# Retention followed by a snake feed-forward layer on one core: later tiles in the natural layout, 64x64 array tiles and a written-out plan

## The chip, the cores and the metric

The kernel runs on one core of one Trainium2 chip. The metric is the device time of one execution in microseconds (us). The changed kernel's time stands against that of the kernel before.

## The reference

Four batches (B), eight heads (H), 768 tokens (S), head size 64 (D). Per batch and head a state of 64x64 decays and takes in one outer product per token; the output is the query times the state. The outputs, heads side by side, are x with 3072 rows of 512, which goes through a feed-forward layer of width 2048.

```
gamma = 1.0 - 2.0 ** (-5.0 - np.arange(H))
for t in range(S):
    state = gamma * state + einsum('bhd,bhe->bhde', k[:, :, t], v[:, :, t])
    y[:, :, t] = 1/sqrt(D) * einsum('bhd,bhde->bhe', q[:, :, t], state)
x = y.transpose(0, 2, 1, 3).reshape(B * S, H * D)
h = x @ w_in
s = sin(alpha * h)
g = h + s * s / (alpha + 1e-09)
out = g @ w_out
```

Inputs and output are float32.

## The kernel before

The tokens are cut into 24 tiles of 128 (six chunks in each of four batches). The list `order` takes the four first chunks first, then the rest batch by batch; "tile n" below is entry n of it. Tiles 0 to 3 are first chunks, 4 to 8 chunks 1 to 5 of batch 0, 9 to 13 those of batch 1, and so on.

**Feed-forward.** Groups of tiles go through it: group 0 has tiles 0 to 3, groups 1 to 10 two tiles each. A `Slot` multiplies w_in's columns of one block f of 128 (two blocks at a time from group 1 on) with the group's x (line 567, `ph`; four matmuls per block), ACT takes the sine (570), ACT or DVE squares (575, 577), DVE adds (582) into `gT`. `ff_out` multiplies `gT` with w_out (592, `po`; 16 matmuls of 512 columns per tile). `ph` and `po` of later groups share four PSUM banks. `phase` runs group g's eight slots between the `po` matmuls of group g-1, and calls the attention of the tiles to come at fixed slots: `score` and `blend` say where, and each tile is spread over a few slots.

**Attention.** A tile needs q and k with the head size on partitions (`qkT`). Tiles 0 to 7 are transposed on PE (`turn_half`, 247 and 249; `half_T`, `stage_T`), tiles 8 and later by a DMA transpose that SyncE issues (`turn`, 284). A *narrow* tile (0 to 9) forms its scores in eight matmuls with 64 rows and 128 columns of the array (`stage_A`, 293); then `stage_M` adds the state's part (332, 128 rows with zeros in `s_bd`), the scores' part (336), and the new state (312). A *wide* tile (10 and later, except first chunks) is loaded with two token halves on one partition and half of the heads in each half of the partitions (`load_seq`); its matmuls use the array as four tiles of 64x64, and `burst` issues one tile's blending, the next one's scores and the state together: `inter` (397), `scores` (413), `part` (433), `mix` (510), 64 small matmuls. Tiles 10 and 14 are wide with whole chunks; the others go in halves of 64 tokens (`fine`). DVE masks the scores (421), adds the state (462, 470), and scales the result into x (`xT`, 528); ACT, for the last batch GpSimd, copies the state to bf16 (438).

**Loads.** GpSimd issues all loads that cast to bf16: `load_chunk` (91, 98: 128 partitions, 64-element pieces), `load_seq` (121: 64 partitions, one head each), `load_w_in` (131) and `load_w_out` (134), four of each over 128 partitions. Its queue also scales v (155) and some decay tables (223). DMAs of this queue go in turn over eight semaphores, so each waits for the landing of the one eight places before. SyncE issues the first q and k, the DMA transposes and the output stores (607), in the order in which they are written.

**Order.** `tc.manual_schedule()` keeps each engine's instructions in the order of the program text: the first part (tiles 0 to 2, with `idle_work` on PE in between), group 0 written out by hand (`w[..]`, `F(ts, lo, hi)`), then the phases.

Of the kernel before, what the change touches and what calls it, by code (L numbers as in the profile page):

```python
# [11 lines left out]
ALU = mybir.AluOpType  # L12


@with_exitstack
def kernel(
# [10 lines left out]

# [37 lines left out]
    w_in_v = moe_w_in.rearrange("(ko ki) f -> ki ko f", ki=128)  # L65
    w_out_v = moe_w_out.rearrange("(fo fi) n -> fi fo n", fi=128)
    raw = {}

# [12 lines left out]
    def load_chunk(j, names="qkv"):  # L81
        for name, src in (("q", q), ("k", k), ("v", v)):
            if name not in names:
                continue
            if name == "v":
                t = big.tile([128, H, D], BF16, name="vr", tag="vr", bufs=10)
            elif name == "q" and paired(j):
                if "pairs" not in raw:
                    raw["pairs"] = work.tile([64, B, H, 2, D], BF16, name="qp", tag="gT", bufs=2)
                t = raw["pairs"][:, order.index(j)]  # L90
                nc.gpsimd.dma_start(out=t.rearrange("i h f d -> i h (f d)"), in_=pairs_of(src, j))
                raw[name, j] = t
                continue
            else:
                if ("qk", j) not in raw:
                    raw["qk", j] = big.tile([128, 2, H, D], BF16, name="qkr", tag="qkr", bufs=9)
                t = raw["qk", j][:, "qk".index(name)]
# [3 lines left out]
    whole = NCH + 2, 2 * NCH + 1  # L101

    def wide(j):
        return j >= NCH + 2 and j % NCH > 0

    def load_seq(bt, names="qkv", hs=range(H)):

        cs = [c for c in range(NCH) if wide(bt * NCH + c)]
        nh = 2 * len(cs)
        if "q" in names and hs[0] == 0:  # L110
            raw["seq", bt] = (big.tile([128, nh, 2, NP, D], BF16, name=f"qk_seq{bt}"),
                              big.tile([128, nh, NP, D], BF16, name=f"v_seq{bt}"))
        tqk, tv = raw["seq", bt]
        for name, src in (("q", q), ("k", k), ("v", v)):
            if name not in names:
                continue
            for h in hs:
                r = slice(64 * (h // NP), 64 * (h // NP) + 64)
                x = h % NP ^ h // NP
                o = tv[r, :, h % NP, :] if name == "v" else tqk[r, :, "qk".index(name), x, :]  # L120
                nc.gpsimd.dma_start(out=o, in_=src[bt, h, cs[0] * C:, :].rearrange("(f i) d -> i f d", i=64))  # L121
        for i, c in enumerate(cs):
            j, f = bt * NCH + c, slice(2 * i, 2 * i + 2)
            raw["qk", j], raw["k", j], raw["v", j] = tqk[:, f], tqk[:, f, 1], tv[:, f]

    WP = 4
    fw = d_ff // WP
    fo = FF // WP

    def load_w_in(i):  # L130
        nc.gpsimd.dma_start(out=w_in[:, :, i * fw:(i + 1) * fw], in_=w_in_v[:, :, i * fw:(i + 1) * fw])

    def load_w_out(i):
        nc.gpsimd.dma_start(out=w_out[:, i * fo:(i + 1) * fo, :], in_=w_out_v[:, i * fo:(i + 1) * fo, :])
# [3 lines left out]
    for name, src in (("q", q), ("k", k)):  # L138
# [4 lines left out]
    nc.sync.dma_start(out=alpha_row, in_=moe_alpha.rearrange("(fo fi) -> fo fi", fi=128))  # L143

    tio = consts.tile([128, C], F32, name="tio")
    nc.gpsimd.iota(tio, pattern=[[1, C]], channel_multiplier=0, base=0, allow_small_or_imprecise_dtypes=True)
    pos = consts.tile([128, NCH], F32, name="pos")
    nc.gpsimd.iota(pos, pattern=[[C, NCH]], channel_multiplier=1, base=0, allow_small_or_imprecise_dtypes=True)


    def scale_v(j, eng):
        t, by = raw["v", j], kg
        if wide(j):
            t, by = t.rearrange("i f p d -> i (f p) d"), kgq
        eng.tensor_mul(t, t, by[:, j % NCH, :, None].to_broadcast([128, H, D]))  # L155

    load_chunk(0, "v")
    load_chunk(order[1])
    load_chunk(order[2])
    load_w_in(0)  # L160
    load_w_in(1)


    warm = consts.tile([128, 512], F32, name="warm")
    nc.vector.memset(warm, 0.0)  # L165
    tiny = consts.tile([128, 1], F32, name="tiny")
    nc.scalar.activation(out=tiny, in_=warm[:, 0:1], func=ACTF.Exp)
    lg = consts.tile([128, H], F32, name="lg")
    for h in range(H):
        nc.vector.memset(lg[:, h:h + 1], lng[h])  # L170
    back = consts.tile([128, H], F32, name="back")
    far = consts.tile([128, C], F32, name="far")
    nc.vector.tensor_scalar(back, lg, pos[:, 0:1], -1.0, op0=ALU.mult, op1=ALU.mult)
    nc.vector.tensor_scalar(far, tio, pos[:, 0:1], 1e6, op0=ALU.is_lt, op1=ALU.mult)
    nc.vector.tensor_scalar_add(back, back, lscale)
    nc.vector.tensor_add(far, far, tio)
    dec = consts.tile([128, 2, NP, C], F32, name="dec")
    for h in range(H):
        nc.scalar.activation(out=dec[:, h % 2, h // 2, :], in_=far, func=ACTF.Exp, scale=lng[h], bias=back[:, h:h + 1])
    ident = consts.tile([128, 128], BF16, name="ident")  # L180
    nc.vector.tensor_scalar(ident, tio, pos[:, 0:1], None, op0=ALU.is_equal)
    lgp = consts.tile([128, NP], F32, name="lgp")
    for p in range(NP):
        for e in range(2):
            nc.vector.memset(lgp[64 * e:64 * e + 64, p:p + 1], lng[2 * p + e])

    expo = consts.tile([128, NCH, H], F32, name="expo")
    nc.vector.tensor_mul(expo, pos[:, :, None].to_broadcast([128, NCH, H]),
                         lg[:, None, :].to_broadcast([128, NCH, H]))
    mask01 = consts.tile([128, 128], BF16, name="mask01")  # L190
    mask_bc = mask01[:, None, :].to_broadcast([128, H, 128])
    kgq = consts.tile([128, NCH, H], F32, name="kgq")
    expoq = consts.tile([128, NCH, H], F32, name="expoq")
    tok = consts.tile([128, NCH, 2], F32, name="tok")
    lgq = consts.tile([128, NP], F32, name="lgq")
    maskq = consts.tile([128, 192], BF16, name="maskq")

    def half_table(b):
        r = slice(64 * b, 64 * b + 64)
        for f in range(2):  # L200
            nc.vector.tensor_scalar_add(tok[r, :, f], pos[r, :], float(64 * (f - b)))
        nc.vector.tensor_copy(lgq[r], lg[r, NP * b:NP * b + NP])

    def later_tables():
        for f in range(2):
            nc.vector.tensor_mul(expoq[:, :, NP * f:NP * f + NP],
                                 tok[:, :, f, None].to_broadcast([128, NCH, NP]),
                                 lgq[:, None, :].to_broadcast([128, NCH, NP]))

    def later_mask():  # L210
        for b in range(2):
            nc.vector.tensor_scalar(maskq[64 * b:64 * b + 64, 0:128], tio[64 * b:64 * b + 64],
                                    tok[64 * b:64 * b + 64, 0, 0:1], None, op0=ALU.is_ge)
        nc.vector.tensor_copy(maskq[:, 128:192], maskq[:, 0:64])
# [5 lines left out]
    nc.vector.memset(cscale, lscale)  # L220
# [5 lines left out]
    nc.vector.tensor_copy(ident_f, ident[:FF, :FF])  # L226
    alpha_sb = consts.tile([128, FF], F32, name="alpha_sb")
    rec_alpha = consts.tile([128, FF], F32, name="rec_alpha")
    s_bd = [big.tile([128, NP, 128], BF16, name=f"s_bd{i}") for i in range(2)]
    s_b = [[big.tile([128, NP, D], BF16, name=f"s_b{i}{f}") for f in range(2)] for i in range(2)]  # L230


    s_f = [big.tile([128, NP, D], F32, name=f"s_f{f}") for f in range(2)]
# [17 lines left out]
    def half_T(j, i, eng):  # L251

        if i == 0:
            st["qkT", j] = work.tile([128, 2 * NP, 128], BF16, name="qkT", tag="qkT", bufs=6)
        pt = psum.tile([128, NP, 128], BF16, name="pt", tag="mm", bufs=4)
        turn_half(j, i, pt)
        leave_T(j, i, pt, nc.scalar.copy if eng is nc.scalar else nc.vector.tensor_copy)

    def leave_T(j, i, pt, copy):

        o = st["qkT", j][:, i * NP:(i + 1) * NP, :]
# [3 lines left out]
        copy(o, pt)  # L265

    def stage_T(j, eng=None, tag="ty"):
        st["qkT", j] = work.tile([128, 2 * NP, 128], BF16, name="qkT", tag="qkT", bufs=6)
        copy = nc.scalar.copy if eng is nc.scalar else nc.vector.tensor_copy
        if paired(j):  # L270
            for i, t in enumerate((tag, "pa")):
                pt = psum.tile([128, NP, 128], BF16, name="pt", tag=t)
                turn_half(j, i, pt)
                leave_T(j, i, pt, copy)
            return
        pt = psum.tile([128, 2 * NP, 128], BF16, name="pt", tag=tag, bufs=4 if tag == "mm" else 1)
        for i in range(2):
            turn_half(j, i, pt[:, i * NP:(i + 1) * NP, :])
        copy(st["qkT", j], pt)

    def turn(j):

        st["qkT", j] = work.tile([128, 2 * NP, 128], BF16, name="qkT", tag="qkT", bufs=6)
        nc.sync.dma_start_transpose(out=st["qkT", j], in_=raw["qk", j].rearrange(
            "i a f p d -> i (a f p d)" if wide(j) else "i a h d -> i (a h d)"))

    def stage_A(j, parts=1):
        qkT = st["qkT", j]
        pa = psum.tile([128, 2, NP, 128], F32, name="pa", tag="pa")
# [5 lines left out]
        aT = work.tile([128, 2, NP, 128], BF16, name="aT", tag="aT", bufs=2)  # L295
        flat = "p e n t -> p (e n) t"
        if parts > 1:
            for h in range(0, NP, NP // parts):
                r = slice(h, h + NP // parts)
# [664 lines left out]
```

## Time and profile before

| what | value |
|---|---|
| three runs | 211.59, 210.24, 210.89 us; median 210.89 |
| span of the profiled execution | 208.4 us; its own time isn't listed apart, the median is 2.5 above the span |
| granted TensorE clock | 1.000 |
| PE busy 0 to 15.2 us | 13.43 us (much of it idle work) |
| PE busy 15.2 to 47 us | 31.08 us of 31.8 |
| PE busy 47 to 181 us | 134.0 us of 134.0 |
| first `ph` matmul | 15.17 us |
| tile 4's transposes on PE | 37.93 us |
| group 1's first slot | 46.72 us |
| GpSimd DMA issues | 72 of `load_seq`, 25 of `load_chunk`, 3 of pairs, 4 + 4 of weights |
| DMA transposes | 16 |

The span runs from the first to the last instruction. Busy shares are means over stages with different limits; PE's matmuls are pipelined, so spans of neighbours overlap, and the distance from start to start is what a matmul costs.

### The profile page before, as it was taken

To read this page: it belongs to the slowest core of one execution; us is meant where nothing else is said; L and a number is where in the kernel's file an instruction comes from. 1 tells how busy PE (TensorE), PEld (TensorE's weight loads), DVE (VectorE), ACT (ScalarE), POOL (GpSimd) and SP (SyncE) were. 2 spreads that over 40 slices of the span, in tenths; PEclk is the share of its full clock that TensorE was granted. 3 is DMA by queue.
4 is the path that set the end of the run, shared out by engine and by line. 5 is a ranking of instruction groups with operands and counts; after the bars stand their busy time and mean duration, and the time that the engine had idled before them with its cause. 6 is when DMAs were issued, how large, how long until landed. Compare 5 with 4: busy or idle time off the path is not lost.

```text
span 208.4 us, 5987 instructions
## 1 busy us (share of the span) xinstructions
PE 202.9 (97%) x2427; PEld 132.3 (63%) x2427; DVE 158.7 (76%) x363; ACT 159.5 (77%) x344; POOL 109.5 (53%) x148
## 2 busy tenths in 40 slices
PE   6998999999999999999999999999999999999994
PEld 2654644567776667666666666666766766666653
DVE  7867897876988597787788778779878778686540
ACT  7858798548997878888888888886787787888821
POOL 8899333898979979999999330000413101000000
PEclk9999999999999999999999999999999999999999
DMA  8999999999999999999999903412415110110112
GB/s 128 156 199 179 201 207 179 155 211 183 132 115 96 193 178 162 170 139 176 174 142 174 173 36 68 101 46 58 104 53 55 53 50 3 53 50 0 50 53 101
DMA packets 98747, 24.78 MB, mean 119 GB/s; under 512 B 91280, under 2 KB 95776, under 8 KB 98720
## 3 DMA queue, kind: packets, MB, share of 16 engines
q0 software_dynamic: 75968, 13.38, 85.6%
q1 hardware_dynamic: 22608, 10.96, 25.0%
q8 instruction: 19, 0.31, 0.6%
q10 hardware_dynamic: 144, 0.07, 0.1%
q14 instruction: 8, 0.07, 0.1%
HBM read 27.27 MB, written 6.29 MB: 161 GB/s over the span
## 4 chain that ended last, share of the span: by engine, by line
PE 94%; DVE 3%; ACT 1%; issue 0%; DVEq 0%
PE ph L567 39%; PE po L592 39%; PE spare L637 3%; PE pa L293 2%; PE poh L617 2%; PE py L397 2%; PE pt L249 1%; PE py L336 1%; PE py L510 1%; PE py L332 1%; PE pa L413 1%; PE pa L433 1%; DVE gT L582 1%; PE ps L312 1%; DVE qkT L265 0%
## 5 line engine op out<-in xcount | busy, mean ns | idle before, releaser
L582 DVE SCALAR_TENSOR_TENSOR gT<-s,rec_alpha,ph 128x256 bf16<-128x256 f32 (+3 forms) x184 | 82.1, 489 | 26.6 <-ACT s L575 25.7
L570 ACT ACTIVATE s<-ph,alpha_sb 128x256 f32<-128x256 f32 (+3 forms) x184 | 79.1, 480 | 29.4 <-PE ph L567 28.3
L567 PE MATMUL ph<-xT,w_in 128*128 128x256 bf16 (+3 forms) x736 | 98.6, 277 | 0.0
L592 PE MATMUL po<-w_out,gT 128*128 128x512 bf16 x368 | 95.3, 380 | 0.0
L567 PEld LDWEIGHTS <-w_in 128*128 128x128 bf16 x736 | 70.5, 98 | 30.4 <-issue 0.4
L575 ACT ACTIVATE s<-s 128x512 f32<-128x512 f32 (+1 forms) x91 | 56.4, 623 | 2.7
L592 PEld LDWEIGHTS <-gT 128*128 128x128 bf16 x368 | 33.9, 98 | 25.9 <-DVE gT L582 0.3
L438 POOL CAST s_b<-s_f 128x256 bf16<-128x256 f32 x10 | 4.0, 399 | 45.4 <-DVE s_f L491 23.6
L121 POOL DMA_DIRECT2D qk_seq<-in_k_dram x24 | 17.1, 762 | 1.5 <-DMA qk_seq<-in_q_dram 1.5
L121 POOL DMA_DIRECT2D qk_seq<-in_q_dram x24 | 17.1, 750 | 1.3 <-issue 0.7
L604 DVE COPY o_sb<-po 128x512 f32<-128x512 f32 x19 | 13.1, 691 | 5.4 <-PE po L592 5.3
L121 POOL DMA_DIRECT2D v_seq<-in_v_dram x24 | 17.1, 785 | 0.0
L155 POOL TENSOR_TENSOR v_seq<-v_seq,kgq 128x512 bf16<-128x512 bf16 x14 | 14.8, 1101 | 4.2 <-DMA v_seq<-in_v_dram 4.2
L637 PE MATMUL spare<-warm 128*128 128x256 f32 (+3 forms) x22 | 10.1, 554 | 1.5 <-DVE warm L165 1.5
L98 POOL DMA_DIRECT2D vr<-in_v_dram x10 | 9.1, 913 | 3.9 <-DMA w_in<-in_moe_w_in_dram 2.0
L421 DVE TENSOR_TENSOR aTw<-pa,maskq 128x512 bf16<-128x512 f32 (+1 forms) x14 | 10.1, 723 | 0.2
L98 POOL DMA_DIRECT2D qkr<-in_k_dram x9 | 8.1, 899 | 3.3 <-DMA w_out<-in_moe_w_out_dram 3.2
L528 DVE TENSOR_TENSOR xT<-py,qg 128x256 bf16<-128x256 f32 x26 | 9.7, 417 | 0.0
L155 POOL TENSOR_TENSOR vr<-vr,kg 128x512 bf16<-128x512 bf16 x8 | 8.7, 1083 | 0.6 <-PE py L336 0.6
L577 DVE TENSOR_TENSOR s<-s 128x512 f32<-128x512 f32 (+1 forms) x7 | 4.4, 633 | 3.8 <-ACT s L570 3.8
L302 DVE TENSOR_TENSOR aT<-pa,mask 128x1024 bf16<-128x1024 f32 x6 | 7.3, 1219 | 0.0
L98 POOL DMA_DIRECT2D qkr<-in_q_dram x6 | 5.4, 896 | 3.6 <-DMA w_in<-in_moe_w_in_dram 2.1
(110 smaller groups left out, 153.0 us busy)
## 6 DMA issues: line engine op xcount, KB each, us to landing
out_dram<-o_sb SPq DMA_DIRECT2D x23, 256.0 KB, 3.0
w_in<-in_moe_w_in_dram POOLq DMA_DIRECT2D x4, 512.0 KB, 9.1
w_out<-in_moe_w_out_dram POOLq DMA_DIRECT2D x4, 512.0 KB, 13.0
vr<-in_v_dram POOLq DMA_DIRECT2D x10, 128.0 KB, 6.3
qk_seq<-in_q_dram POOLq DMA_DIRECT2D x16, 80.0 KB, 6.3
qk_seq<-in_k_dram POOLq DMA_DIRECT2D x16, 80.0 KB, 4.6
v_seq<-in_v_dram POOLq DMA_DIRECT2D x16, 80.0 KB, 3.8
qkr<-in_k_dram POOLq DMA_DIRECT2D x9, 128.0 KB, 7.1
```

Source lines behind the costliest of these rows:

```text
L98: nc.gpsimd.dma_start(out=t, in_=chunk_of(src, j))
L121: nc.gpsimd.dma_start(out=o, in_=src[bt, h, cs[0] * C:, :].rearrange("(f i) d -> i f d", i=64))
L155: eng.tensor_mul(t, t, by[:, j % NCH, :, None].to_broadcast([128, H, D]))
L421: nc.vector.tensor_mul(aT.rearrange("p e m t -> p e (m t)").rearrange("p e (n t) -> p e n t", t=t), pa[:, :, 0:2 * n].rearrange("p e (n t) ...
L528: nc.vector.tensor_mul(x[:, 2 * b:2 * b + 2, :], y.rearrange("p (m t) -> p m t", m=2), qg[:, c, 2 * b:2 * b + 2])
L567: nc.tensor.matmul(self.ph[:, m, :], w_in[:, i, f * 128:(f + 1) * 128], xT[g][:, i, self.lo:self.hi], start=(m == 0 and i == 0), stop=(i = ...
L570: nc.scalar.activation(out=self.s[:, m, :], in_=self.ph[:, m, :], func=ACTF.Sin, scale=alpha_sb[:, f:f + 1])
L575: nc.scalar.activation(out=self.s, in_=self.s, func=ACTF.Square)
L582: nc.vector.scalar_tensor_tensor(gT[self.g][:, f, self.lo:self.hi], self.s[:, m, :], rec_alpha[:, f:f + 1], self.ph[:, m, :], op0=ALU.mult ...
L592: nc.tensor.matmul(po[g, ts], gT[g][:, f, ts * C:(ts + 1) * C], w_out[:, f, :], start=(f == 0), stop=(f == FF - 1))
L604: nc.vector.tensor_copy(o_sb, po[g, ts])
L637: nc.tensor.matmul(spare["ps"][:, :m], warm[:, :128], warm[:, :m], start=True, stop=True)
```

## The change

The narrow way falls away for all tiles but the four first chunks, and `load_seq` with it. Tiles 4 to 23 are loaded by `load_chunk` with tokens on partitions; the two token halves of a tile are the two halves of the partitions, and each is a chunk of its own in 64x64 array tiles. A burst is now: the blending of the old tile's one half (`blend(old, 0)`, 16 small matmuls), the new tile's scores (`products4`, 16) and states of both halves (`sums`, 16), the blending of the other half (16). The first tile of a batch adds 16 for the first chunk's state; for batch 0 that state is `opening` (8 matmuls). Half of x's heads come out on the other half of the partitions (`seat`, `slanted`), and w_in's rows are loaded to match: `load_w_in` issues four DMAs of 64 partitions where one had 128. Tile 7 is transposed by DMA, not on PE. The order up to and with group 3's slots is one list, `PLAN`; from group 4 on `phase` issues slots, bursts (in slots 1 and 5) and `O` pieces in the pattern of before.

The PLAN's words: `S:f:tag:lo:hi:i:j` matmuls of block f for tiles lo to hi and row blocks i to j; `S:g.n` slot n of group g, `sin`, `sq`, `add` its parts; `F:ts:f` and `O:g:ts:f` `po` matmuls; `TP`/`Tp` transposes on PE, `CP`/`Cp` their copies; `turn:n` DMA transpose; `A`, `K`, `M`, `X` the first chunks' scores, decay, product and exit; `W`, `w` the opening; `B:old:new:first` a burst, `E:mask|keep|exit` what DVE and ACT do of it; `sv` scales v; `ld`, `wi`, `wo` loads; `take` stores; `tab`, `bm` tables.

```diff
-    w_in_v = moe_w_in.rearrange("(ko ki) f -> ki ko f", ki=128)
+    w_in_v = moe_w_in.rearrange("(b k u r) f -> u b r k f", b=2, u=2, r=64)
...
-        nc.gpsimd.dma_start(out=w_in[:, :, i * fw:(i + 1) * fw], in_=w_in_v[:, :, i * fw:(i + 1) * fw])
+        for u in range(2):
+            for x in range(2):
+                nc.gpsimd.dma_start(out=w_in[half(x), 2 * u:2 * u + 2, c], in_=w_in_v[u, x ^ u, :, :, c])
...
+    def blend(j, turned, fresh=False):
+        py, c = st["py", j], j % NCH
+        qkT, aT, vs, s = st["qkT", j], st["aT", j], raw["v", j], s_b[c % 2]
+        for n in range(4):
+            i = n % 2
+            for bank in range(2):
+                r = bank ^ turned
+                for x in range(2):
+                    own = (n < 2) ^ (bank == 1)
+                    e = r if own else (r if bank == 0 else 1 - r)
+                    f = e ^ bank
+                    p = i + 2 * (e ^ x)
+                    o = py[bank][half(x), 128 * e + 64 * i:128 * e + 64 * i + 64]
+                    if own:
+                        w, m = s[f][half(r), p, :], qkT[half(r), p, half(f)]
+                    else:
+                        w, m = vs[half(r), 2 * p + e, :], aT[half(r), e, p, 0:64]
+                    ins = nc.tensor.matmul(o, w, m, start=(fresh and n == 0), stop=True, skip_group_check=True)
+        return ins
...
     def burst(old, new, first=None):
+        if first is not None:
+            sums(first, py, True)
+        if old is not None:
+            st["py", old] = py
+            last = blend(old, 0, first is None)
+        if new is not None:
+            more["mask"] = products4(new)
+            pa = st["pa"]
+            sums(new, [pa[:, b, :] for b in range(2)])
+        if old is not None:
+            behind(nc.tensor.nop(), last)
+            blend(old, 1)
```

The PLAN from just ahead of tile 4's transposes to tile 9's scores, GpSimd's words left out:

```
F:2:1:mm F:0:9:ps F:0:10:ps F:0:11:ps sin:15 sq:15:A TP:4:pa CP:4:A tab:4:V bm sq:13:V add:13 sq:12:V add:12 F:1:12:ty F:0:12:ps
F:0:13:ps add:14 F:0:14:ps F:2:2:mm W:0:mm turn:7 sv:4:V add:15 B::4: w:A E:keep:4 F:1:13:ty F:1:14:ty F:1:15:ty E:mask:4 TP:5:mm take:0:1:A
F:0:15:ps F:3:0:mm CP:5:V take:0:0:A F:2:3:mm F:2:4:mm F:2:5:mm F:2:6:mm F:2:7:mm sv:5:V B:4:5: E:mask:5 F:2:8:mm TP:6:mm CP:6:A E:exit:5 F:2:9:mm
F:2:10:mm F:2:11:mm F:2:12:mm F:2:13:mm F:2:14:mm E:keep:5 B:5:6: turn:8 turn:9 F:2:15:mm take:0:2:A E:exit:6 E:keep:6 F:3:1:mm F:3:2:mm F:3:3:mm
S:1.0:mm sin:1.0 S:1.1:mm sin:1.1 E:mask:6 sq:1.1:A S:1.2:mm F:3:4:mm B:6:7: sq:1.0:V add:1.0 sin:1.2 add:1.1 sq:1.2:A E:keep:7 F:3:5:mm S:1.3:mm
F:3:6:mm sin:1.3 S:1.4:mm sq:1.3:A F:3:7:mm F:3:8:mm F:3:9:mm F:3:10:mm sin:1.4 E:exit:7 F:3:11:mm F:3:12:mm E:mask:7 sq:1.4:A F:3:13:mm add:1.2
add:1.3 B:7:8: E:keep:8 add:1.4 S:1.5:mm sin:1.5 E:mask:8 S:1.6:mm sq:1.5:A E:exit:8 S:1.7:mm F:3:14:mm add:1.5 sin:1.6 sq:1.6:V F:3:15:mm sin:1.7
B:8:9:1 take:0:3:A
```

In SyncE's queue the order is tile 7's transpose, two output stores, the transposes of tiles 8 and 9, two stores, tile 10's transpose, and so on.

More of the change, by code (lines that the diff above doesn't have):

```diff
@@ L533, in burst @@
-    def burst(old, new, first=None):
-        inter(old)
-        now = old if old % NCH < NCH - 1 else first
-        more = scores(new) if new is not None else {}
-        if now is not None:
-            more.update(state(old, now, new))
-        more.update(mix(old, now is None))
-        if now is not None and not wide(now):
-            more.update(state_rest(old, now))
-        return more
-    def run(more, *kinds):
-        for kind in kinds:
-            if more and kind in more:
-                more.pop(kind)()
+        for p in range(NP):
+            for b in range(2):
+                for e in range(2):
+                    nc.tensor.matmul(pa[half(b), e, 64 * p:64 * p + 64], qkT[half(e), NP + p, half(b)],
+                                     qkT[half(e), p, half(b)], start=(p == 0), stop=True, skip_group_check=True)
@@ new lines, in products4, with sums @@
+        st["aT", j] = aT = work.tile([128, 2, NP, 64], BF16, name="aTw", tag="aT", bufs=2)
+        def mask():
+            nc.vector.tensor_mul(aT, pa[:, :, 0:256].rearrange("s e (p t) -> s e p t", t=64),
+                                 maskq[:, None, None, :].to_broadcast([128, 2, NP, 64]))
+        return mask
+    def sums(j, to, first=False):
+        ks, vs = raw["k", j], raw["v", j]
+        for p in range(NP):
+            for b in range(2):
+                for e in range(2):
+                    nc.tensor.matmul(to[b][half(e), 256 + 64 * p:320 + 64 * p], ks[half(b), 2 * p + e, :],
+                                     vs[half(b), 2 * p + e, :], start=(first and p == 0), stop=True, skip_group_check=True)
@@ L935 @@
+    emit(PLAN.split())
+    emit(steady())
+    emit(f"O:{NG - 1}:{ts}:{f}" for ts in range(sizes[-1] - 1) for f in range(FF))
     last_tile(NG - 1, sizes[-1] - 1)
```

854 lines of the change are left out of this document (272 added, 582 removed).

## The prediction, made before the changed kernel was run

> **What bounds the kernel now.** I read the page first (engines, slices, chain), then PE in order of time, then the DMA issues with their times to landing, then the queues of GpSimd and SyncE.
>
> ```profile
> span 208.4 us, 5987 instructions
> PE 202.9 (97%) x2427; PEld 132.3 (63%) x2427; DVE 158.7 (76%) x363; ACT 159.5 (77%) x344; POOL 109.5 (53%) x148
> PE   6998999999999999999999999999999999999994
> DMA  8999999999999999999999903412415110110112
> PE 94%; DVE 3%; ACT 1%; issue 0%; DVEq 0%
> ```
>
> PE carries 94% of the chain; DVE and ACT have a quarter of the span free. So time is won by taking work from PE or by closing its gaps, and the gaps lie before about 45 us. The DMA engines are full until 115 us, so there a load or a DMA transpose arrives at a time that PE cannot hasten.
>
> ```profile
> 51.07 1.04 PE L567 MATMUL ph<-xT,w_in 128*128 128x256 bf16 x8
> 52.03 0.41 PE L332 MATMUL py<-qkT,s_bd 128*64 128x128 bf16 x8
> 52.28 0.39 PE L336 MATMUL py<-aT,vr 128*64 128x128 bf16 x8
> 52.50 0.29 PE L312 MATMUL ps<-vr,qkr 128*64 128x64 bf16 x8
> 52.73 0.40 PE L293 MATMUL pa<-qkT 64*128 64x128 bf16 x8
> 53.06 0.60 PE L592 MATMUL po<-w_out,gT 128*128 128x512 bf16 x2
> ...
> 93.45 1.04 PE L567 MATMUL ph<-xT,w_in 128*128 128x256 bf16 x8
> 94.42 0.32 PE L397 MATMUL py<-qkT,s_b 64*64 64x64 bf16 x16
> 94.57 0.30 PE L413 MATMUL pa<-qkT 64*64 64x64 bf16 x16
> 94.69 0.30 PE L433 MATMUL pa<-v_seq,qk_seq 64*64 64x64 bf16 x16
> 94.82 0.40 PE L510 MATMUL py<-aTw,v_seq 64*64 64x64 bf16 x16
> 95.15 1.04 PE L592 MATMUL po<-w_out,gT 128*128 128x512 bf16 x4
> ```
>
> The starts give the prices, since spans overlap. Eight 128x256 ph with nothing behind them take 0.87 (91.72 to 92.59), four 128x512 po 0.86: 0.108 and 0.216 each. A narrow tile's attention (51.07 to 53.06, less 0.87) is 1.12, and L332, L336 and L312 without scores 0.79 (54.80 to 56.46); I take 1.15 a tile. A wide tile's burst of 64 small matmuls is 95.15 - 93.45 - 0.87 = 0.83.
>
> The DMA issues, three stretches of the trace (47 to 49, 50 to 52, 131 to 133 us):
>
> ```profile
> out_dram<-o_sb SPq DMA_DIRECT2D x1, 256.0 KB, 5.4
> qkT<-qkr SPq DMA_TRANSPOSE x1, 8.5
> ...
> qkT<-qkr SPq DMA_TRANSPOSE x1, 10.2
> ...
> qkT<-qk_seq SPq DMA_TRANSPOSE x1, 3.1
> ```
>
> The last column is us from issue to landing: a DMA transpose alone takes 3.1, amid full queues and behind a store 8.5 and 10.2; one at 64.3 with loads beside it took 6.0.
>
> **The sum.** The span is 208.4. The page lists no separate time for the profiled execution; the runs' median, 210.89, is 2.5 above the span, and I carry these 2.5 over unchanged.
>
> *Start, -0.9.* Before, the last attention matmuls of tile 2 stand at 14.19, idle work follows, and ph begins at 15.17 with 384 columns. The PLAN begins ph directly behind the same matmuls, on tiles 0 and 1 (256 columns) and then tile 2. The path to them is the same: q of tile 2 lands at 4.87 + 5.2 = 10.07 in the same place of the queue. First ph at about 14.3; w_in's first quarter lands at 7.28 + 7.4 = 14.7, its first pieces earlier. Between -1.0 and 0.
>
> *From there to tile 4's transposes, +1.4.* Before: from 15.17 to 37.93, 22.8 us for 22.0 of PE work, 0.8 lost. After, the waits by rows: w_in's second quarter lands at 8.06 + 9.1 = 17.2, and columns f 0 to 2 are through by 16.5 (0.7); tile 3's transposes wait for loads that land at 18.1 and 18.75 (0.15); its second attention step waits for the 1.22 DVE multiply with 0.9 of PE work put between instead of 1.4 (0.4); the slots of f 13 and the first po of the third tile wait for DVE, which has a table (0.67), two mask pieces (0.28 each) and a square (0.69) ahead of their adds (0.7); matmuls cut in two cost 0.15. That is 2.1 less 0.8. Between 0 and +2.5.
>
> *Attention on PE, -2.3.* Away: six narrow tiles at 1.15 = 6.9, two opening states at 0.25 = 0.5, tile 7's eight transposes (0.45): 7.85. Come: six bursts at 0.83 = 5.0, one of them cut in two 0.25, the opening 0.3: 5.5. The later bursts hold 64 small matmuls before and after, so nothing changes there; each four of the new order names four different quarters of the array, as L397 does, so I keep 0.83. Between -2.8 and -1.8. With it go the waits of 38 to 47 us before (0.6, against 0.2 that I find after): -0.4.
>
> *Tiles 7, 8, 9 through SyncE, +3.1.* This is the term that decides. Adding the PLAN's items from tile 4's transposes (37.6) at these prices, PE reaches the scores of tile 7 at 50.0, of tile 8 at 54.4, of tile 9 at 58.4; before, PE turned tile 7 itself at 46 and wanted tiles 8 and 9 at 60.5 and 65.1. The loads come in the same order to k of tile 7, which lands at 38.42 + 6.8 = 45.2. Its transpose, at the front of SyncE's queue, then takes 6.0 (the row at 64.3): 51.2, 1.2 late. SyncE stands at that wait, so the first two output stores queue behind it and in front of tile 8's transpose: k at 48.0 plus 8.5 to 9 gives 57.0, and PE, already 1.2 late, waits 1.4 more. Tile 9: k lands at 51 to 52 (50.6 before, but now a transpose and two stores share the engines from 45 on), plus 10: 61.5, another 0.5. Between 0 (3.1 to 4.6 each, as late in the trace) and +5.5 (10.2 for each behind the stores: 63.9).
>
> *Hidden.* GpSimd's loads fall from 72 at 0.76 to 42 at 0.89 (55 to 37 us); the 12 more w_in issues (some 8.5 us) come where GpSimd waits for the DMA eight places before anyway (2.07 and 2.00 us in its queue at 25.39 and 30.68); without that cover tile 4's load and all behind it slip by what is late. Scaling v is 24 times as before. DVE and ACT have the same work per later tile (mask 0.69, two adds 0.42, two exits 0.42, two copies 0.39); only from 43 to 58 do three bursts meet eight slots, 15.6 us of DVE: full, and were the tiles early, DVE would give 58.6.
>
> *Sum:* -0.9 + 1.4 - 2.3 - 0.4 + 3.1 = +0.9. The other way round: from tile 9's scores on PE has 72 slots at 0.868 (62.5), 304 po (65.6), the last tile 3.55 and attention 13.0: 144.6. From 61.5 it ends at 206.1, against 205.4 before: +0.7. The balance is at 60.8. I take +0.8: **211.7**.
>
> **Rivals.** *The tiles are there in time.* For it: a lone transpose took 3.1 to 4.6, and after 48 GpSimd issues loads more slowly than the engines take them. Against: slices 9 to 23 show full DMA engines. PE meets tile 9 at 58.5: 205.4 - 2.3 = 203.1 at PE's end, 208.5. [...]
>
> *The transposes queue up, slower.* In SyncE's one queue tile 7's transpose, two stores, tile 8's and tile 9's follow each other: before, store, transpose, transpose landed at 52.5, 56.4, 60.9, so about 4.2 a transpose and 2 a store: 51.5, 55.5, 59.7, 64. From 64: +3.2, 214.1. It decides from 61.5 on for tile 9. For it: 10.2 was reached with less ahead. Against: with the loads gone a store and a transpose issued together landed within 3.1, so not all of their time adds up.
>
> *Half the partitions, half the rate.* The new w_in loads write 64 partitions each. Were each to run at half the rate, a quarter would take 5.0 instead of 17.2 - 14.7 = 2.5, the second land at 22.2, and PE stand 4.5 there in place of 0.7: 211.7 + 3.8 = 215.5. Against: the 64-partition qp landed in 5.2, the 128-partition qkr after it in 5.1. [...]
>
> **Chances.** Waits eat the gain (210 to 213): 0.40; in time (207 to 209.5): 0.28; queued up (213 to 216): 0.24; half rate (214 to 217): 0.08. One per cent, 2.1 us, is about what a measurement of this kernel can tell from no change; the bounds are 208.8 and 213.0. Faster: 0.25 of the second and 0.03 of the first (the start term at its best); slower: 0.22 of the third, 0.08, and 0.09 of the first (the early waits at their worst). Faster 0.28, same 0.33, slower 0.39. The likeliest case alone spans 209.5 to 213.2; the range 207.5 to 215.5 leaves out little but the ends of the two outer cases.
>
> **What would show it.** First ph at 14.3 and tile 4's transposes near 37.6: start and early waits. Gaps of PE at about 50, 56 and 61 in front of the 64x64 scores of tiles 7, 8, 9, released by a DMA on qkT: the deciding term; no gap there means the first rival, gaps of 3 us and more the second. Bursts of 0.83 from 40 us on: the PE saving. w_in's pieces landing after 18 us: the third. I am wrong altogether if PE waits for DVE or ACT in the phases after 75 us, or if the 64x64 groups of the new order take clearly over 0.83.

## Result and the profile after

The changed kernel takes 218.7 us (218.59 to 219.7), the kernel before 210.89: a ratio of 1.038, 95% interval 1.034 to 1.041. It is slower by 7.8 us, and 7.0 above the 211.7 of the prediction, outside its range. The profiled execution took 218.74, 1.7 more than its span. Times here and below are medians of a kernel's executions; the ratios leave out the few that took over 1.5% more than the kernel's fastest.

The page of the changed kernel (busy time, slices of TensorE and of its granted clock, shares of the chain):

```profile
span 217.0 us, 6524 instructions
...
PE 204.6 (94%) x2691; PEld 135.7 (63%) x2691; DVE 158.4 (73%) x365; ACT 157.6 (73%) x340; POOL 104.3 (48%) x130
...
PE   6899699999679999999999999999999999999994
...
PEclk9999999999957999999999999999999999999999
...
PE 72%; POOL 15%; DMA 11%; issue 1%; DVE 0%; POOLq 0%
```

PE's share of the chain fell from 94% to 72%; GpSimd and the DMA now hold 26%. PE's slices from 54 to 65 us stand at 6 and 7, the one from 22 to 27 us at 6, and in two slices (60 to 71 us) the granted clock is at 5 and 7. Before, no slice of PE but the first and the last was under 8, and the clock stood at 9 throughout. PE in order of time (start, us, form, count; in brackets idle time just before, and its releaser):

```profile
24.93 0.81 PE L446 MATMUL po<-w_out,gT 128*128 128x512 bf16 x3 [1.55 <-DMA w_out<-in_moe_w_out_dram]
...
39.45 0.90 PE L202 MATMUL pt<-ident,qk 128*128 128x128 bf16 x8
...
53.23 0.32 PE L315 MATMUL pa<-qkT 64*64 64x64 bf16 x16 [0.38 <-DMA qkT<-qk]
...
57.54 0.22 PE L305 MATMUL py<-qkT,s_b 64*64 64x64 bf16 x2
...
61.16 0.43 PE L315 MATMUL pa<-qkT 64*64 64x64 bf16 x16 [3.31 <-DMA qkT<-qk]
...
61.95 5.30 PE L417 MATMUL ph<-xT,w_in 128*128 128x256 bf16 x24
...
67.97 0.30 PE L315 MATMUL pa<-qkT 64*64 64x64 bf16 x16
```

The gap that decides stands at tile 8, where the prediction put 1.4 us: 3.31. What it did not have at all is the line behind it: 24 ph take 5.1 us from start to the next start (61.95 to 67.05) instead of 2.6. The windows by stage (us, busy us of PE, PEld, DVE, ACT, POOL, then granted clock, DMA share, GB/s) show why:

```profile
57.00:60.00 3.00, 0.85 (x19) 0.30 (x17) 0.62 (x2) 1.04 (x3) 2.52 (x3) 1.00 3.50 118
60.00:62.00 2.00, 0.84 (x49) 0.78 (x50) 0.15 (x1) 0.00 (x0) 0.38 (x1) 0.61 2.73 102
62.00:67.20 5.20, 5.20 (x29) 3.73 (x26) 3.90 (x10) 2.71 (x6) 5.19 (x6) 0.50 2.25 172
67.20:75.00 7.80, 7.80 (x131) 5.44 (x129) 6.46 (x14) 6.19 (x14) 6.54 (x9) 0.99 2.09 181
```

The clock was granted at 0.50 from 60.5 us, still inside the gap of 3.31 us, to about 67.2. The prediction, whose own sum had no gap over 1.4, did not look at the clock.

The transposes of tiles 7, 8 and 9 (last column: us from issue to landing), from three stretches at 48.5, 51.9 and 58.2 us:

```profile
qkT<-qk SPq DMA_TRANSPOSE x1, 4.6
...
qkT<-qk SPq DMA_TRANSPOSE x1, 9.3
...
qkT<-qk SPq DMA_TRANSPOSE x1, 8.9
```

They took 4.6, 9.3 and 8.9; 6.0, 8.5 to 9, and 10 were forecast. So it is less the length of the transposes that was off than their start. The chain of what ended last says where that came from (start, us, what):

```profile
13.59 1.05 POOL qg L181
...
17.05 7.84 DMA w_out<-in_moe_w_out_dram
...
26.45 1.05 POOL qg L181
...
28.25 2.26 POOL v L158 x2
...
31.29 1.05 POOL qg L181
32.34 1.75 POOL qk L130 x2
34.10 0.89 POOL v L130
...
44.43 1.75 POOL qk L130 x2
...
47.05 1.08 POOL v L158
...
51.85 9.27 DMA qkT<-qk
...
62.02 5.24 PE ph L417 x24
```

From 13.6 to 48 us the chain runs through GpSimd's queue and one DMA of it: w_out's first quarter is issued at 17.05 (14.89 before), then come two tables and two scalings (26.45 to 32.3, with w_out's last two quarters between them), and only then tile 4's loads, each 0.89, one behind the other. k of tiles 7, 8 and 9 are issued at 42.66, 45.25 and 51.48; before it was 38.42, 40.22 and 43.20.

### The profile page after: what moved, and what is told of

Its sections match the earlier page's. It is cut to its first block, busy times and chain, and to the rows that moved or that the text cites. A ratio compares the mean times of both kernels' runs of the same rounds, so it can differ in the third digit from the quotient of the medians.

```text
span 217.0 us, 6524 instructions
## 1 busy us (share of the span) xinstructions
PE 204.6 (94%) x2691; PEld 135.7 (63%) x2691; DVE 158.4 (73%) x365; ACT 157.6 (73%) x340; POOL 104.3 (48%) x130
## 4 chain that ended last, share of the span: by engine, by line
PE 72%; POOL 15%; DMA 11%; issue 1%; DVE 0%; POOLq 0%
PE ph L417 33%; PE po L446 32%; POOL qk L130 5%; DMA qkT<-qk 4%; DMA w_out<-in_moe_w_out_dram 4%; PE py L305 4%; POOL v L130 3%; DMA v<-in_v_dram 3%; POOL v L158 2%; PE poh L462 2%; POOL qg L181 1%; PE pa L331 1%; PE pa L315 1%; POOL qp L123 1%; POOL w_in L138 1%; POOL w_out L141 1%
## 5 line engine op out<-in xcount | busy, mean ns | idle before, releaser
L437 DVE SCALAR_TENSOR_TENSOR gT<-s,rec_alpha,ph 128x256 bf16<-128x256 f32 (+3 forms) x184 | 81.7, 488 | 29.0 <-ACT s L430 28.3
L158 POOL TENSOR_TENSOR v<-v,kg 128x512 bf16<-128x512 bf16 x21 | 23.3, 1113 | 18.9 <-DMA v<-in_v_dram 18.8
L130 POOL DMA_DIRECT2D v<-in_v_dram x24 | 21.3, 890 | 2.0 <-DMA qk<-in_q_dram 1.2
L130 POOL DMA_DIRECT2D qk<-in_k_dram x23 | 20.6, 897 | 0.0
L130 POOL DMA_DIRECT2D qk<-in_q_dram x20 | 18.4, 918 | 0.0
L371 DVE TENSOR_TENSOR xT<-py,qg 128x256 bf16<-128x256 f32 x40 | 14.9, 414 | 1.2 <-PE py L305 1.2
L320 DVE TENSOR_TENSOR aTw<-pa,maskq 128x512 bf16<-128x512 f32 x20 | 13.6, 682 | 0.5 <-PE pa L331 0.5
L305 PE MATMUL py<-qkT,s_b 64*64 64x64 bf16 x320 | 12.8, 197 | 0.2 <-PE py L305 0.2
L305 PE MATMUL py<-aTw,v 64*64 64x64 bf16 x320 | 12.2, 198 | 0.0
L305 PEld LDWEIGHTS <-s_b 64*64 64x64 bf16 x320 | 9.0, 108 | 4.8 <-issue 2.5
L386 DVE TENSOR_TENSOR s_f<-s_f,pa 128x256 f32<-128x256 f32 x20 | 8.3, 416 | 5.0 <-PE pa L331 4.9
L138 POOL DMA_DIRECT2D w_in<-in_moe_w_in_dram x16 | 9.7, 630 | 4.6 <-DMA w_out<-in_moe_w_out_dram 3.0
```

The lines of the kernel that those rows point to most:

```text
L130: nc.gpsimd.dma_start(out=t, in_=chunk_of(src, j))
L138: nc.gpsimd.dma_start(out=w_in[half(x), 2 * u:2 * u + 2, c], in_=w_in_v[u, x ^ u, :, :, c])
L158: eng.tensor_mul(t, t, kg[:, j % NCH, :, None].to_broadcast([128, H, D]))
L305: ins = nc.tensor.matmul(o, w, m, start=(fresh and n == 0), stop=True, skip_group_check=True)
L320: nc.vector.tensor_mul(aT, pa[:, :, 0:256].rearrange("s e (p t) -> s e p t", t=64), maskq[:, None, None, :].to_broadcast([128, 2, NP, 64]))
L371: nc.vector.tensor_mul(slanted(x, bank), py[bank][:, 0:256].rearrange("p (e k t) -> p e k t", e=2, k=2), slanted(qg[:, c], bank))
```

## Experiments

Ratios are to the kernel before on the same chip, with 95% intervals; the changed kernel stands at 1.038. The kernel before took 210.6 to 211.5 us beside these runs.

**1. Tiles 7, 8, 9 turned by TensorE.** In the PLAN:

```
- turn:7 ... turn:8 turn:9
+ TP:7:mm CP:7:V (before S:1.0)  TP:8:mm CP:8:A (before S:1.4)  TP:9:mm CP:9:V (before F:3:15)
```

> The changed kernel with tiles 7, 8 and 9 turned by TensorE instead of by SyncE's transposing DMAs. Theory (the turned tiles come late): the 3.3 us wait at 57.9 and the half clock behind it (61 to 67 us) go, eight transposes a tile (0.45 each, 1.35 in all) come; tile 9's scores at 62 to 63 instead of 67.97, the time 213 to 214. Rival (ScalarE and VectorE are 6.7 and 6.3 of 7 us busy from 50 to 57, and the copies of 0.7 to 1.0 each come on top): the wait only changes its releaser, gain under 2, 217. Rival (the loads themselves are what is late): k of tile 9 lands at 58.2, so the wait moves to the transposes of tile 9, which then stand at 58.5 or later; tile 8's, whose k landed at 51.3, do not wait.

Measured: 215.1, 1.018 (1.014 to 1.021); the clock stays at 1.00. Tile 9's scores come at 64.14. PE in order of time:

```profile
56.07 1.03 PE L417 MATMUL ph<-xT,w_in 128*128 128x256 bf16 x8 [1.65 <-DVE gT L437]
...
62.75 0.61 PE L202 MATMUL pt<-ident,qk 128*128 128x128 bf16 x8 [0.54 <-DVE gT L437]
...
64.14 0.32 PE L315 MATMUL pa<-qkT 64*64 64x64 bf16 x16 [0.19 <-DVE qkT L231]
```

Without the DMA transposes the kernel gains 4 us net, as the theory has it by sign, though not the 5 that it named; 2.2 us are lost to waits for VectorE, which holds up group 1's slots: the first rival is right in part. Of the profiled execution alone, 1.1 us is no effect of the edit: tile 4's transposes, ahead of anything that it touches, stand at 38.34 there and at 39.45 in the changed kernel.

**2. TensorE kept busy in the wait for tile 8.** Ahead of the scores of tile 8:

```
+ for n in (512, 512, 512, 256): nc.tensor.matmul(pa[:, 0, :n], warm[:, :128], warm[:, :n], start=True, stop=True)
```

> The changed kernel with four matmuls of no use (128 columns of zeros by 512, 512, 512, 256, some 3.0 us at the full clock) put into TensorE's wait for tile 8's transposes, into a bank that the scores then overwrite. Theory A (the clock costs what it slows): the granted clock stays at 1.00 from 61 to 67 us, the 24 ph take 2.6 instead of 5.1, nothing else waits: 216.2. Theory B (tile 9's transposes land at 67.1 whatever TensorE does): PE is at tile 9 at 65.4 and waits there for 1.7 us, so only 0.8 is won, 217.9, and the clock was no cost of its own.

Measured: 217.9, 1.026 (1.019 to 1.034), the figure of B, but the interval holds A's as well, and the executions lie apart, 215.0 to 219.3. In the profiled one, the fastest, tile 8's transpose was there after 6.3 us, as the fillers began, and they were in vain. So the clock's own price is not shown: tile 9's transposes landed at about 58.2 + 8.9 = 67.1 in the changed kernel, so that a full clock could have won 0.9 at most. What is shown is that the landing moves: behind the same two stores the transpose took 9.3 us in the changed kernel's execution and 6.3 in this one.

**3. The kernel before, w_in in 16 DMAs**, of 64 partitions each, and of 128:

```
+ for u, x in 2 x 2: w_in[64x:64x+64, 2u:2u+2, c]      (halves)
+ for u in 4:        w_in[:, u:u+1, c]                 (whole)
- w_in[:, :, c]
```

> The kernel before with w_in loaded in 16 DMAs of 128 KB that write 64 partitions each (as in the changed kernel) instead of 4 of 512 KB on 128; order of the loads and rows as before. Theory A (the number of DMAs: each waits for the one eight places before it, so fewer bytes are ahead of the engines): tile 4's loads and transposes come 1 to 2 us later, 212 to 213, and 16 whole-partition DMAs do the same. Theory B (64 partitions load slower): 1 us or more slower than the 16 whole-partition DMAs. Theory C: hidden, 210.9.

> The kernel before with w_in in 16 DMAs of 128 KB on all 128 partitions (one of the four row blocks each; rows of 1 KB in both). Theory A (the number of DMAs): the same as the 16 halves, 212 to 213. Theory B (the partitions): 210.9 to 211.5 while the halves are slower. Theory C: hidden, 210.9 for both.

Measured: 215.05, 1.016 (1.012 to 1.020), and 214.7, 1.017 (1.011 to 1.024). The number costs 3 to 4 us, twice what theory A named, the partitions nothing. In the kernel of whole partitions PE waits for what is queued behind w_in (its waits: us in total, times, longest):

```profile
PE po L594 <- DMA w_out<-in_moe_w_out_dram: 2.4, 1, 2.4
...
PE pt L251 <- DMA qkr<-in_k_dram: 1.0, 1, 1.0
```

GpSimd issued that kernel's first quarter of w_out at 17.82 (14.89 before), and tile 4's q at 29.03 (19.30). Its queue, before and then in the kernel of whole partitions (start, us):

```profile
7.28 1.56 POOL L131 DMA_DIRECT2D w_in<-in_moe_w_in_dram  x2
...
14.89 0.78 POOL L134 DMA_DIRECT2D w_out<-in_moe_w_out_dram  x1
```

```profile
7.27 2.75 POOL L133 DMA_DIRECT2D w_in<-in_moe_w_in_dram  x5
...
17.82 0.78 POOL L136 DMA_DIRECT2D w_out<-in_moe_w_out_dram  x1
...
26.26 1.20 POOL L133 DMA_DIRECT2D w_in<-in_moe_w_in_dram  x2 [3.71 <-DMA w_out<-in_moe_w_out_dram]
```

The first eight of the 16 issues take 4.3 us in all (2.75 and three of 0.53) where two took 1.56: that is 2.8 of the 2.9 us by which w_out is issued later; waits are 0.7 us of that stretch, 0.58 before. The other eight take 2.9 us more than their two, and a wait of 3.71 for the late w_out comes on top: 9.7 at tile 4's q. The waits of 1.3 to 2.1 us that stood behind it before then take back about half: tile 7's k is issued at 43.04, before at 38.42. A part of the price is the clock, which falls to 0.50 in both profiled executions (21.8 to 25.1 us with the halves, 27 to 30.5 with whole partitions; the mean over the span is 0.992 in each); how much is not shown.

**4. The changed kernel with 4 plain DMAs for w_in** (`w_in[:, :, c]` from plain rows), alone and with experiment 1. These kernels leave out the swap of half of w_in's rows, so that their sums pair other rows than they should; the other instructions are the same.

> The changed kernel with w_in in 4 DMAs of 512 KB on all partitions, its rows in the plain order; the swap of half of the rows is left out, so that the hidden sums pair other rows than they should; the instructions are otherwise the same. Theory (the number of w_in's DMAs is what makes everything behind them late, by 3.5 us as in the kernel before): first ph at about 14.5, no wait for w_out at 24.9, tile 4's transposes at 37.6 to 38, k of tile 7 at 45 to 46; the transposes of tiles 7 to 9 then come as forecast and the time is 211.7 to 214. Rival (the transposing DMAs take 8 to 9 us whenever they start, and the clock halves behind the wait): tile 8 still waits 3 us and more, 215 to 216.

> The same (4 plain DMAs, the swap of w_in's rows left out), and tiles 7, 8 and 9 turned by TensorE as in the run before. Theory: both causes are gone and what is left are the terms -0.9 (start), +1.4 (early waits), -2.3 (attention), -0.4, and 1.35 for the added transposes: about 210, and up to 211.5 where the wait of 1.65 us for VectorE at 56 stays. Rival (a third cause, in the bursts after 68 us, 0.84 each where the kernel before has 0.77): 1 us more, 211 to 212.5.

Measured: 218.8, 1.038 (1.035 to 1.042), and 218.1, 1.036 (1.032 to 1.039): no gain. Both expectations failed, in part on a collision. Three lines of the first kernel, of VectorE, GpSimd and TensorE:

```profile
18.97 2.96 DVE L430 TENSOR_TENSOR s<-s 128x384 f32<-128x384 f32 x1 [0.34 <-ACT s L423]
```

```profile
19.09 2.05 POOL L156 TENSOR_TENSOR v<-v,kg 128x512 bf16<-128x512 bf16 x2
```

```profile
23.05 0.40 PE L242 MATMUL pa<-qkT 64*128 64x128 bf16 x8 [2.37 <-DVE qkT L218]
```

The same square took 0.56 in the changed kernel. With fewer DMAs, GpSimd reached its scalings of v 9 us earlier, just as VectorE squared, and PE waited 2.4 us for tile 3's scores; the clock then fell to 0.50 (25 to 28 us; the mean over the span is 0.992). The second kernel also waits 2.4 us for VectorE's `gT`.

**5. The scalings of v of tiles 1 and 2 moved** behind the loads of tiles 11 and 14 (`sv:1:G`, `sv:2:G`), with 4 plain DMAs and with the 16:

> The kernel of 4 plain w_in DMAs (the swap of half of w_in's rows left out) with GpSimd's scalings of v of tiles 1 and 2 moved behind the loads of tiles 11 and 14. Theory (in the run of 4 plain DMAs the two scalings, 19.1 to 21.1 us, met VectorE's square of 19.0, which took 2.96 us instead of 0.56 and held up tile 3's copy, TensorE by 2.4 us and its clock): the square takes 0.56, tile 3's scores come at 20.5 to 21 instead of 23.05, tile 4's transposes at 38 to 39 instead of 42.4; the time 213 to 215. Rival (the number of w_in's DMAs doesn't matter in this order of loads, and something else holds up the first 40 us): tile 4's transposes stay after 40, 217 or more.

> The changed kernel with one thing moved: GpSimd's scalings of v of tiles 1 and 2 (2.3 us) behind the loads of tiles 11 and 14. With the run of the same queue and 4 plain DMAs for w_in (216.96) it tells what the number of DMAs is worth in this order of loads. Theory (the 16 DMAs keep GpSimd waiting for the DMA eight places before, so w_out and tile 4 come late): the wait for w_out at 24.9 and tile 4's transposes at 39 to 39.5 stay, against 37.4 with 4 DMAs; loads 2.3 us earlier, tile 8 waits 1 us instead of 3.3, 215 to 217.5. Rival (the number of DMAs costs nothing here): tile 4's transposes at 37 to 38.

Measured: 217.0, 1.028 (1.023 to 1.034), and 218.3, 1.031 (1.023 to 1.039). (The first again leaves out the swap of w_in's rows.) In the first the square is back at 0.56, which bears the collision out, but the time is above the 213 to 215 that was expected. Tile 4's transposes stand at 37.37 in the first and at 39.98 in the second (the changed kernel: 39.45): the number of DMAs is worth up to 2.6 us there (0.85 of them stand already at the first ph, 14.97 and 15.82). In the end the two ratios can't be told apart, for tile 9 waits 2.97 in the first and 2.56 in the second, and in the second the clock then falls (its slice from 65 to 70 us stands at 6, the mean over the span is 0.990).

**6. The stores behind tile 8's transpose**, then also tile 9's q and k ahead of a scaling:

```
- take:0:1 and take:0:0 store at once ... turn:8 turn:9        + turn:8 put:1 put:0 turn:9
- sv:7:G ld:qkv:9                                              + ld:qk:9 sv:7:G ld:v:9    (second kernel only)
```

> The changed kernel with the first two output stores behind tile 8's transpose in SyncE's queue instead of in front of it. Theory (the stores ahead in the queue make tile 8's transpose last 9.3 us): issued at 51.4 it lands in 4.6 to 6, at 56 to 57.4; no wait at 57.9, the clock stays at 1.00 in 61 to 67, tile 9 comes at 64 to 67 as its k lands at 58.2 and the stores are now ahead of it: 215 to 217.5. Rival (the loads that fill the engines make it late): still 8 us and more, 218 to 219.

> The changed kernel with the first two output stores behind tile 8's transpose (as in the run before) and q and k of tile 9 loaded ahead of GpSimd's scaling of v of tile 7, which waits 1.5 us for that v to land. Theory (tile 9's wait of 4.8 us came from its k, issued 8.3 us later than in the kernel before, and from the stores now ahead of it): k of tile 9 is issued at 48 to 49 and lands at 55, its transpose at 61 to 63; the wait falls to 0.5 to 2 us, the clock stays, 214 to 216. Rival (the transposes share the engines, and tile 9's is as late whenever its k lands): 218.

Measured: 218.7, 1.037 (1.034 to 1.041), then 215.2, 1.023 (1.014 to 1.031). In the first, tile 8's transpose is in time (its scores stand at 56.58 with no wait; the median of the kernel's 17 transposes is 5.6 us, in the changed kernel 8.8), and tile 9 pays instead:

```profile
56.58 0.30 PE L315 MATMUL pa<-qkT 64*64 64x64 bf16 x16
...
65.56 0.43 PE L315 MATMUL pa<-qkT 64*64 64x64 bf16 x16 [4.79 <-DMA qkT<-qk]
```

So the stores in front help to make tile 8's transpose late, as the theory says (experiment 2 has 6.3 behind them, so not all of the 9.3 is theirs), but taking them away alone moves the wait. Tile 9's came from its k, which stood behind a scaling that waits 1.5 us for v of tile 7: with both moves the waits are 2.7 (tile 7) and 0.6 (tile 9).

**7. GpSimd's queue as a whole**: three tables and two scalings behind loads, w_in's last 8 blocks in 4 DMAs, and the second move of 6.

> The changed kernel with GpSimd's queue in another order: its three tables and the scalings of v of tiles 1 and 2 (5.4 us) behind the loads of tiles 5, 7, 8, 10 and 14 instead of ahead of tile 4's, w_in's last eight columns of blocks in 4 DMAs of 256 KB instead of 8, q and k of tile 9 ahead of the scaling of v of tile 7. Theory (GpSimd is what makes the loads of tiles 4 to 9 late: from 25 to 49 us it is busy without a pause, with tables and scalings between the DMAs): k of tiles 7, 8 and 9 land 3, 3 and 8 us earlier, at 45 to 46, 48 and 50 to 52; the waits for the turned tiles and the half clock go; tile 9's scores at 60 to 62, the time 211 to 213. Rival (the engines are full, so what is issued earlier only lands as late): 216 and more.

Measured: 217.8, 1.035 (1.030 to 1.040). No DMA transpose is waited for any more, as the theory has it, yet the time is not won: PE waits 2.94 for the larger w_in DMAs at 28.3, the clock drops behind it (a mean of 0.86 from 30 to 40 us), and in the middle of a burst PE stands 2.31 with no releaser. Moved in one piece, the order brought other waits. A variant with one idle filler of PE less ahead of tile 2's scores was expected to have its first ph at 14.7 to 14.9 and to win 0.3 to 0.7 us. It had it at 14.46, against 14.66 in this kernel, and its four executions took 213.9 to 220.3, so that nothing can be told of the 0.3 to 0.7; PE again stood 2.58 in the middle of a burst with no releaser.

**8. The second half of py moved out of the burst** (the no-op and `blend(old, 1)` behind the next po):

> The changed kernel with the second half of each burst's py (the no-op that waits for the first half, and its 16 matmuls) moved behind the next matmuls of phase 3 (one token of the PLAN, four po in the written-out loop), and the keeping of the state behind it. Theory (TensorE stands 0.1 us at the no-op, since only 32 small matmuls lie between the halves): each burst falls from 0.84 to about 0.77, 16 of them, -1.1: 217.6. Rival (the order of the small matmuls costs it): still 0.84, or more as small and large matmuls change more often: 218.7 to 220.

Measured: 221.3, 1.049 (1.046 to 1.052), above the rival's 218.7 to 220. The profiled execution took 518.8, so only the times of the other three can be read. The theory's gain is refuted; what makes this order slower, the turns between small and large matmuls or the state that is kept later, is not shown.

**9. The moves together**: both of 6 and the scalings of 5; then tile 7 turned by TensorE as well; then the tables ahead of tile 3's and tile 4's loads moved too; and that with 4 plain DMAs.

> The three moves that leave every instruction as it is, together: the first two stores behind tile 8's transpose, q and k of tile 9 ahead of the scaling of v of tile 7, the scalings of v of tiles 1 and 2 late. Theory (the turned tiles are late because of where GpSimd and SyncE stand, not because a transpose takes long): tiles 7, 8 and 9 come 2 us earlier than with the first two moves (215.2), the waits there (3.3 in all) fall to 1 or less: 212 to 214. Rival (transposes that follow each other share the engines with the loads and take 7 us each however early): 214.5 to 215.5.

> The same, and tile 7 turned by TensorE as in the kernel before (eight transposes, 0.45 us, one copy on VectorE of 0.7). Theory (with tile 7's transpose in flight, tile 8's behind it makes both late: 7.5 us for tile 7's in the run of the first two moves): tile 7's wait goes, tiles 8 and 9 have SyncE's queue to themselves: 211.5 to 213.5, the fastest of the changed kernel's forms. Rival (VectorE, 6.3 of 7 us busy there, makes a slot wait as it did with three tiles turned): no faster than the run beside it.

> The changed kernel with all moves that helped: stores behind tile 8's transpose, q and k of tile 9 ahead of the scaling of v of tile 7, scalings of v of tiles 1 and 2 late, tile 7 turned by TensorE (the run of these: 213.2), and now GpSimd's first table ahead of tile 3's loads moved behind tile 5's, its third behind the scaling of v of tile 6. Theory (the table of 1.05 us ahead of tile 3's loads and of w_out's first quarter is half of the wait for w_out, 1.1 to 2.1 us at 24): that wait falls to 0 to 1, 212 to 213, within 1% of the kernel before. Rival (the engines are full from 8 to 40 us, so w_out lands as late whoever is moved): 213.2 and more.

> The same with w_in in 4 plain DMAs of 512 KB (the swap of half of its rows left out). Theory (the 16 DMAs still cost what they cost in the kernel before, less what the other order hides): 1 to 2 us less than the run beside it, 210 to 212, so that the number of DMAs is the rest of the loss. Rival (with GpSimd's queue in the new order it is hidden): the same as the run beside it.

Measured: 215.2, 1.019 (1.012 to 1.026); 213.2, 1.011 (1.002 to 1.019); 213.3, 1.010 (1.006 to 1.014); 211.55, 1.001 (0.998 to 1.004). The last kernel leaves out the swap of w_in's rows, as in 4. The late scalings add nothing to 6, and the first kernel's time is its rival's. With tile 7 off SyncE's queue the next two are in time (tile 9 waits 0.3). The table moves show no further gain. The last two ran side by side: the 16 DMAs cost 1.8 us even in this order. From the changed kernel to the last, 7.2 us are won back: 5.4 by the order of the queues and by tile 7's transposes on PE, 1.8 by the number of DMAs. No form is faster than the kernel before. The third kernel's profiled execution, its fastest, took 211.36 (the median is 213.3); behind the first 2 us PE waits nowhere for more than 0.8, and it meets tiles 4, 8 and 9 at 38.59, 56.04 and 60.70, where the prediction had 37.6, 57.0 and 61.5:

```profile
38.59 0.61 PE L202 MATMUL pt<-ident,qk 128*128 128x128 bf16 x8
...
51.51 0.30 PE L315 MATMUL pa<-qkT 64*64 64x64 bf16 x16
...
56.04 0.30 PE L315 MATMUL pa<-qkT 64*64 64x64 bf16 x16
...
60.70 0.32 PE L315 MATMUL pa<-qkT 64*64 64x64 bf16 x16 [0.37 <-DMA qkT<-qk]
```

## Why the prediction was wrong, step by step

PE's stands against the forecast: tile 4's transposes 39.45 for 37.6 (1.85 late), tile 8's scores 61.16 for 57.0 (2.3 more), tile 9's 67.97 for 61.5 (2.3 more), the end 213.94 for 206.1 (1.4 more); outside the span 0.8 less. Together 7.0.

- **"Hidden": a step that failed.** The 12 more w_in issues were costed at nothing, as they were to come where GpSimd waits anyway, at 25.39 and 30.68. They come earlier: eight of the 16 stand ahead of w_out's first quarter, where the kernel before waits 0.58 us. In experiment 3 their bare issue time makes w_out 2.9 us late, and the wait for that late w_out adds 3.7. The engines have less to move meanwhile: in the changed kernel they moved 156, 121 and 167 GB/s in three windows of 3 us from 14 to 23 us, before 185, 183 and 204, together 0.38 MB less. Everything behind slips, as the prediction wrote for the case without cover. Experiment 3 prices it at 3 to 4 us in the kernel before; in the changed kernel 9 prices it at 1.8, and in 5 it is within the noise.
- **Tiles 7 to 9, +3.1: the step that failed by most; right mechanism, wrong clock time.** "The loads come in the same order to k of tile 7": they do, but not at the same time, and it was to land at 45.2. Between w_out and tile 4's loads the PLAN puts two tables and two scalings (4.4 us; before, nothing), on top of the late w_out, and k of tile 9 behind a scaling that waits. The k's landed near 48.6, 51.3 and 58.2, not at 45.2, 48.0 and 51 to 52. The order of GpSimd's queue was to be read there, not the sum of its instructions. The moves in the two queues and tile 7 on PE won 5.4 us (experiment 9, third kernel).
- **The clock** was missing. Its half rate is shown (0.50 from 60.5 to about 67.2 us), its price on top of tile 9's late transposes is not (at most 0.9).
- **Start, -0.9, and +1.4 to tile 4.** First ph came at 15.48 instead of 14.3, behind four idle matmuls (1.1 us) in front of tile 2's scores. Kernels with the same start have it between 14.55 and 15.82, so this term was smaller than its own spread. That is 1.2 of the 1.85 at tile 4. The other 0.65 is what is left of a wait of 1.55 for w_out, which the +1.4 lacked, while other waits of that term were shorter than forecast; that wait would have met an earlier start all the sooner (14.84 in the second kernel of experiment 6, and w_out waited for at 24.07).
- **Attention, -2.3: nearly right.** PE's busy time in the repaired execution is 201.6 with tile 7's transposes (0.45) in it, before 202.9: -1.75. The rest is mostly the later bursts, said to stay as they are. They take 0.84 (124.35 to 126.06, less 0.87), before 0.77 (124.53 to 126.17):

```profile
125.47 0.30 PE L315 MATMUL pa<-qkT 64*64 64x64 bf16 x16
125.59 0.30 PE L331 MATMUL pa<-v,qk 64*64 64x64 bf16 x16
125.81 0.22 PE L305 MATMUL py<-qkT,s_b 64*64 64x64 bf16 x2
...
126.06 1.04 PE L446 MATMUL po<-w_out,gT 128*128 128x512 bf16 x4
```

Between the 16 sums (125.59) and the next py (125.81) lie 0.22 us, before 0.12 (125.77 to 125.89). That the no-op between them is the cause is only argued: experiment 8 could not show it.
- **Small waits, -0.4:** right, one wait of 0.24 from 40 to 50 us.
- **Rivals.** Tiles in time: refuted. Half partitions: refuted as a rate (experiment 3: 215.05 with the halves, 214.7 with whole partitions; no run shows the half rate that it took), though in the kernel before w_in did cost about the 3.8 us that it named, by number. Queued up (214.1): right in sign and in the stores' part (experiment 6), but it put the fault in SyncE's queue alone. By the prediction's own signs the gap of 3.31 at tile 8 spoke for this rival.
- **The forecast figure and the mended kernel.** The last kernel of experiment 9 takes 211.55, next to the 211.7. That is luck: it waits 1.0 us for the turned tiles in place of 3.1, and about what it saves there is lost at the start (first ph at 15.22, not 14.3) and in the later bursts (0.07 each).

## What to carry to other kernels

A load cut in four is not free: its issues take the queue's time (0.53 to 0.6 us each here), and whatever stands behind them is late by that, so look whether the waits that are to cover them come before or after. Where each DMA waits for one a fixed number of places before, a late DMA then holds up the next ones too (3.71 us in experiment 3). When a consumer needs a tile by a given time, follow that tile's own issue down its queue, with every table, scaling and wait in front of it; moving one wait away can move it to the next tile until the queue itself is mended (3.31 us at tile 8 became 4.79 at tile 9 in experiment 6). And before adding up late arrivals, ask what a gap of 2 to 3 us does to the clock (here 0.50 behind some of them, 1.00 behind others).

## What the hardware showed beyond the expected

- In a PE gap of 3.31 us the granted clock fell to 0.50, about 2.65 us after the gap began (57.85 to 60.5), and stayed there for the next 5.9 us of work (61.16 to 67.05). Gaps of 1.67 (experiment 3, halves, with one of 0.50 just before), 2.11 (experiment 9, second kernel), 2.37 (3, whole) and 2.56 (5, second kernel) were followed by 0.50 too (means over the span, in this order: 0.992, 0.991, 0.992, 0.990); gaps of 2.68 (6, second kernel) and 2.97 (5, first kernel) were not, the clock stayed at 1.00. So in these executions the length of a gap alone does not tell whether the clock falls behind it.
- GpSimd held VectorE up: a square of 0.56 took 2.96 beside two scalings of together 2.05, which were no longer than elsewhere (two took 2.26 in the changed kernel). The square's record starts 0.12 us before theirs and ends 0.8 us after them; with the scalings moved (experiment 5, first kernel) it takes 0.56 again. By what means GpSimd held it up is not shown.
- A DMA transpose behind the same two stores landed after 6.3 us in one execution (experiment 2) and 9.3 in another (the changed kernel).
- PE stood 2.31 us in the midst of a burst (experiment 7) with no releaser in the profile, and 2.58 in the variant with one filler less. Why PE stood stays open.
